# Three early operands of a mixed stage get buffers of their own, and the tiles around them move

## The chip, the cores and the metric

The kernel runs on one core of a Trainium2 chip. The metric is the device time of one execution in microseconds; lower is better. TensorE (PE) multiplies matrices into PSUM banks, VectorE (DVE), ScalarE (ACT) and GpSimd (POOL) work element by element, and SyncE (SP) and POOL issue transfers (DMA). The engines run their own programs in order and wait for each other by semaphores.

## The reference

```python
def reference(**kwargs):
    ...
    attn_out = _attn_ref(**attn_kwargs)
    B, H, S, D = attn_out.shape
    x = np.ascontiguousarray(attn_out.transpose(0, 2, 1, 3)).reshape(B * S, H * D)
    x = _moe_ref(x=x, **moe_kwargs)
    return _moe2_ref(x=x, **moe2_kwargs)
```

Attention here is a decaying linear state, `state = gamma * state + k v^T`, read with q, over 4 x 8 heads of 768 steps. Its 3072 rows of 512 go through `h = (x @ w1) * (x @ w2)`, `h @ w3`, `@ w_out`, and then through `h = x @ w_in`, `g = h * sigmoid(1.702 h)`, `g @ w_out`. All of it is float32.

## The kernel before

Every float32 product is made of three products of a reduced format: `mm3` multiplies high by high (L246), low by high (L247) and high by low (L248). The high part is a cast on ACT (L261, L132), the low part a subtraction on DVE (L162). Matrix products are also done by a scheme of seven products on 2 x 2 blocks, so the program has products P1 to P7 and sums of blocks. The program is written out by hand under `manual_schedule`: every engine runs in the order of the code. The tile pools hold SBUF addresses; where a new tile lies over older ones, its first writer waits for the last users of each of those tiles.

The order of stages is attention, with the first gates in it; the **gated blocks** (`ORDER = (0, 2, 4, 1, 3, 5)`, 8 steps `t` of 24 matmuls each), beside which the weights are mixed; the **mixed stage** (`blend`, 21 turns of 24 matmuls); **Expand**; and a contraction.

In the gated blocks n = 3 to 5, `gate_second` makes, for each pair of steps, `b12` and five quantities `g`, from two quantities `b` that an earlier block stored to `hd`. `b` is loaded with `load_b` (L1011), `g` is stored with `hd<-g` (L1027). DVE computes L1021 and L1024, POOL L1025 and L1026. In the last gated block, `opening(t)` also loads the first weights (`load_wm`) and the first operands of the mixed stage (`load_h`, tile names h0, h1), splits h0 and two weights into high and low.

In a turn of `blend`, PE multiplies operand n; ACT then makes the high part of operand n + 1 (`split_h`) and of the weight n + 2, and DVE the low parts; and `copied` on ACT takes finished banks (P1, P5, P6) into values `s`. P4's banks are copied to tiles "c" (tag `o`). POOL stores both to `yd`. Operands are loaded by `load_turn` (L796) three turns ahead. The pool of `blend` is named "c" and reuses addresses of the gated block. Expand's tiles (s, u, g, b) then reuse addresses of `blend`; its ACT copies at L551 take PE's banks a and e to s1, s5, u2 and so on.

Tile names carry a buffer number in the program's lists (`l_3865`); m, a, e and psm are PSUM banks.

Of the kernel before, what the change touches and what calls it, by code (L numbers as in the profile page):

```python
# [7 lines left out]
F32 = mybir.dt.float32  # L8
F32R = mybir.dt.float32r
# [7 lines left out]
P = 128  # L17
# [4 lines left out]
TB = 512  # L22
NB = NT // TB
# [3 lines left out]
R_BUFS = 5  # L27
# [10 lines left out]
NM = KF // 2  # L38
# [5 lines left out]
def tile_kernel(  # L44
# [242 lines left out]
    def h_tile():  # L287
        return xs.tile([P, 2, TB], F32, tag="h", bufs=2, name="h")
# [13 lines left out]
    class Attention:  # L302
# [9 lines left out]
        def tile(self, kind, n, bufs):  # L312
            return self.pool.tile([P, n], F32, tag=kind, bufs=bufs, name=kind)
# [479 lines left out]
    def load_h(n, a, b, t):  # L793
        i, name = blends[n]
        lo2.setdefault(n, []).append((a, b, t))
        nc.sync.dma_start(t.bitcast(F32), hd[i][:, a:b, RIGHT[name]])  # L796
# [13 lines left out]
    def split_wm(n):  # L810
        hi, lo = wm[blends[n][1]]
        split(hi, lo, lo.bitcast(F32))

    def load_wm(n):
        name = blends[n][1]
        wm[name] = wtile("wg")
        nc.sync.dma_start(wm[name][1].bitcast(F32), sm[PART[name]].rearrange("p k c -> p (k c)"))

    def opening(t):
        if t in range(1, 5):  # L820
            load_wm(t - 1)
        if t == 1:
            x = spare.tile([P, 7, TB], F32R, tag="ope", name="h0")
            hi2[0] = x[:, NM:]
            load_h(0, 0, NM, x[:, :NM])
        if t == KF - 2:
            for k in (0, 2):
                load_h(1, k, k + 2, prep.tile([P, 2, TB], F32R, tag="r", bufs=R_BUFS, name="h1"))
        if t in (3, 4, 5):
            split_h(0, t - 3, t - 2, hi2[0][:, t - 3 : t - 2])  # L830
        if t == 6:
            hi2["k3"] = prep.tile([P, TB], F32R, tag="x", bufs=6, name="h3")
            split_h(0, 3, 4, hi2["k3"].rearrange("p (a t) -> p a t", a=1))
        if t in (4, 6):
            split_wm(t // 2 - 2)

    def blend(p, ps, todo):
        ws = {}

        def tile(kind, bufs):  # L840
            return p.tile([P, NM, TB], F32R, tag=kind, bufs=bufs, name=kind)

        def load_turn(n):
            if n < len(blends):
                load_h(n, 0, NM, ls.pop(n) if n in ls else tile(f"l{n % 4}", 1))

        def value():
            return p.tile([P, TB], F32, tag="s", bufs=8, name="s")

        def copied(ps):  # L850
            t = ready.pop() if ready else value()
            nc.scalar.copy(t, ps)
            return t

        def store(i, e, t):
            nc.gpsimd.dma_start(yd[i][:, e], t)

        ls = {n: tile(f"l{n % 4}", 1) for n in range(2, 6)}
        load_turn(2)
        for n in range(4, 7):  # L860
            load_wm(n)
        load_turn(3)
        held = [p.tile([P, TB], F32, tag="o", bufs=2, name="c")]
        hi2[1] = tile("h", 2)
        ready = [value()]
        for n, (i, name) in enumerate(blends):
            if n < 7:
                ws[name] = [x.rearrange("p (k c) -> p k c", k=NM) for x in wm[name]]
            if n:
                load_turn(n + 3)  # L870
            if name == "P1":
                a, e, c = ([None] * 2 for _ in range(3))
                kept = [{}, {}]
            bank = dict(P5=e, P3=e, P2=c).get(name, a)
            for q in range(2):
                if name in ("P1", "P5", "P2"):
                    bank[q] = ps.tile([P, TB], F32, tag="m", bufs=8, name="m")
                for k in range(NM):
                    mm3(
                        bank[q],  # L880
                        *(x[:, k, q * P : (q + 1) * P] for x in ws[name]),
                        hi2["k3"] if (n, k) == (0, 3) else hi2[n][:, k],
                        low_h(n, k),
                        k == 0 and name in ("P1", "P5", "P2"),
                        k == NM - 1,
                    )
            if n == 7:
                left_tile(0)
                fetch_left(0)
            if n + 1 < len(blends):  # L890
                if n:
                    hi2[n + 1] = tile("h", 2)
                split_h(n + 1, 0, NM, hi2[n + 1])
            if n + 2 < 7:
                split_wm(n + 2)
            todo(n)
            for q, x in enumerate(kept):
                m = bank[q]
                if name in ("P1", "P5", "P6"):
                    x[name] = copied(m)  # L900
                if name == "P2":
                    nc.vector.tensor_tensor(x["P1"], m, x["P1"], ALU.add)
                    store(2 * i, q, x["P1"])
                if name == "P7":
                    nc.vector.tensor_tensor(x["P5"], m, x["P5"], ALU.add)
                    store(2 * i + 1, 2 + q, x["P5"])
                if name == "P3":
                    nc.vector.tensor_tensor(x["P6"], m, x["P6"], ALU.add)
                    store(2 * i + 1, q, x["P6"])
                if name == "P4":  # L910
                    t = held.pop() if held else p.tile([P, TB], F32, tag="o", bufs=2, name="c")
                    nc.scalar.copy(t, m)
                    store(2 * i, 2 + q, t)

    with tc.manual_schedule():
# [54 lines left out]
        with (  # L970
# [35 lines left out]

            hb = []

            def load_b(i, k):
                t = h_tile()  # L1010
                nc.sync.dma_start(t, hd[i // 2][:, k, :2])  # L1011
                hb.append(t)

            def gate_second(t, i, ab):
                nonlocal b12, g
                b = hb[0]
                if t % 2 == 0:
                    b12 = first_b.pop() if first_b else b12_tile()
                    g = pb.tile([P, 5, TB], F32, tag="g", bufs=2, name="g")
                    gate_out(b12, ab)  # L1020
                    nc.vector.tensor_tensor(g[:, 1], b12, b[:, 0], ALU.subtract)  # L1021
                    return
                gate_out(g[:, 0], ab)
                nc.vector.tensor_tensor(g[:, 3], g[:, 0], b12, ALU.subtract)  # L1024
                nc.gpsimd.tensor_tensor(g[:, 2], g[:, 0], g[:, 1], ALU.subtract)  # L1025
                nc.gpsimd.tensor_tensor(g[:, 4], b[:, 1], g[:, 2], ALU.subtract)  # L1026
                nc.gpsimd.dma_start(hd[i // 2][:, t // 2, 2:], g)  # L1027
                hb.pop(0)

            def b12_tile():  # L1030
                return pb.tile([P, TB], F32, tag="b", bufs=2, name="b12")
# [2 lines left out]
            for n, i in list(enumerate(ORDER))[1:]:  # L1034
                nxt = ORDER[n + 1] if n + 1 < NB else None
                for t in range(KF):
                    if nxt is None:
                        opening(t)
                    elif t < 2:
                        for d in range(2):  # L1040
                            reload(nxt, 2 * t + d)
                    if n > 2 and t % 2 == 0 and t + 2 < KF:
                        load_b(i, t // 2 + 1)
                    if n >= 2 and nxt is not None and t == KF - 2:
                        load_b(nxt, 0)
                    ab = gate_mm(t, i, gate_tile)
                    if nxt is not None and t in range(KD - 1, KF - 1):
                        split_x(nxt, t - KD + 1)
                    work(((8, 6, 3, 3)[n - 1] + (n < 4) * (t % 2)) if n < 5 else (t < 4) + (t < 5))
                    (gate_second if n > 2 else gate_first)(t, i, ab)  # L1050
                    while rows < KF and (complete > W3 + rows or (n, t) == (2, KF - 1)):
                        ps = mix_mm(rows)
                        work(7)
                        mix_out(rows, ps)
                        rows += 1
                        if rows == KF:
                            stage.close()
                            pb = homes["st"] = stage.enter_context(
                                tc.tile_pool(name="b2", bufs=1, reuse_waits="tile")
                            )  # L1060
                            st_ready = [pb.tile([P, 1024], F32, tag="st", bufs=2, name="st")]
                            first_b = [b12_tile()]
                            pb.tile([P, 1024], F32, name="gap")
        inner.close()
        homes["st"] = second.enter_context(
            tc.tile_pool(name="wa", bufs=1, side="right", reuse_waits="tile")
# [135 lines left out]
```

## Time and profile before

| what | value |
|---|---|
| median of three runs | 982.17 us (981.41 to 983.0) |
| span of the profiled execution, its own time | 982.2 us |
| PE busy | 963.9 us, 98% |
| DVE, ACT, POOL busy | 718.7, 443.9, 203.3 us |
| mean granted clock of PE | 0.998 |
| mixed stage begins, Expand begins | 397.06, 515.92 us |

The span is from the first to the last instruction of one profiled execution. It equals the median, so its times need no scaling.

### The profile page before, as it was taken

The page shows a single profiled execution, that of the slowest core. Times are in us where ns is not written, and L with a number is a line of the kernel's source. Part 1 is how long each engine was busy: PE and PEld are TensorE (multiplying, and loading weights), DVE is VectorE, ACT ScalarE, POOL GpSimd, SP SyncE. Part 2 cuts the span into 40 slices and gives each one's busy share as a digit, 9 for nine tenths or more (in the row PEclk, how much of TensorE's full clock was granted, in tenths as well). Part 3 has the DMA queues.
Part 4 walks back from the last instruction along what each step waited for, and adds up shares of the span by engine and source line. Part 5 has one row for each costly group of instructions (what it writes and reads, how often), then busy time and mean ns, then how long its engine had stood idle before and what let it go on. Part 6 is the DMA issues. An engine that isn't in the chain of part 4 may idle for free.

```text
span 982.2 us, 14858 instructions
## 1 busy us (share of the span) xinstructions
PE 963.9 (98%) x5608; PEld 835.2 (85%) x5608; DVE 718.7 (73%) x965; ACT 443.9 (45%) x787; POOL 203.3 (21%) x248
## 2 busy tenths in 40 slices
PE   7899999999999999999999999999999999999998
PEld 6788878888888888788889999999999888888886
DVE  4878878989898996765786895867777475567662
ACT  5666644443322222545536745444545544354430
POOL 5010000278685875250110000000000000000000
PEclk9999999999999999999999999999999999999999
DMA  9889965669998989979868647465596968767871
GB/s 362 347 325 355 354 208 192 220 232 346 319 318 324 347 316 356 402 254 322 269 233 296 242 176 278 174 235 223 202 360 253 331 227 282 244 192 251 288 236 54
DMA packets 115288, 268.73 MB, mean 274 GB/s; under 512 B 8000, under 2 KB 69440, under 8 KB 106128
## 3 DMA queue, kind: packets, MB, share of 16 engines
q1 hardware_dynamic: 100688, 193.98, 56.6%
q0 software_dynamic: 14384, 73.61, 19.2%
q8 instruction: 44, 0.72, 0.3%
q14 instruction: 28, 0.23, 0.1%
q10 hardware_dynamic: 144, 0.20, 0.1%
HBM read 165.52 MB, written 102.24 MB: 273 GB/s over the span
## 4 chain that ended last, share of the span: by engine, by line
PE 88%; DVE 5%; DMA 3%; ACT 2%; issue 1%; POOL 0%; DVEq 0%; ACTq 0%; POOLq 0%
PE m L247 11%; PE m L248 11%; PE m L246 11%; PE psm L246 7%; PE psm L247 7%; PE psm L248 7%; PE a L247 4%; PE a L248 4%; PE a L246 4%; PE e L248 2%; PE e L247 2%; PE e L246 2%; PE y L404 2%; PE s L354 2%; PE psg L246 1%
## 5 line engine op out<-in xcount | busy, mean ns | idle before, releaser
L246 PE MATMUL psm<-xh,wh 128*128 128x512 f32 x320 | 124.6, 389 | 0.0
L247 PE MATMUL psm<-xl,wh 128*128 128x512 f32 x320 | 124.5, 389 | 0.0
L248 PE MATMUL psm<-xh,wl 128*128 128x512 f32 x320 | 124.5, 389 | 0.0
L246 PE MATMUL m<-h,op 128*128 128x512 f32 x320 | 124.5, 389 | 0.0
L248 PE MATMUL m<-h,op 128*128 128x512 f32 x320 | 124.5, 389 | 0.0
L247 PE MATMUL m<-l,op 128*128 128x512 f32 x304 | 118.3, 389 | 0.0
L685 ACT CAST h<-l 128x2048 fp32r<-128x2048 f32 x38 | 72.3, 1914 | 83.0 <-PE m L248 58.0
L686 DVE TENSOR_TENSOR l<-l,h 128x2048 fp32r<-128x2048 f32 x38 | 85.6, 2286 | 20.7 <-ACT h L685 20.7
L247 PE MATMUL a<-yl,op 128*128 128x384 f32 x256 | 85.6, 334 | 0.1
L246 PE MATMUL a<-yh,op 128*128 128x384 f32 x256 | 85.6, 334 | 0.0
L248 PE MATMUL a<-yh,op 128*128 128x384 f32 x256 | 85.5, 334 | 0.0
L691 POOL DMA_DIRECT2D op<-sw x6 | 3.2, 533 | 393.2 <-PE a L248 212.9
L128 ACT ACTIVATE x<-raw 128x512 f32<-128x512 f32 x72 | 46.6, 672 | 76.1 <-DMA raw<-in_wo_dram 43.9
L246 PEld LDWEIGHTS psm<-xh,wh 128*128 128x128 f32 x320 | 60.1, 188 | 12.7 <-issue 0.2
L248 PEld LDWEIGHTS psm<-xh,wl 128*128 128x128 f32 x320 | 60.1, 188 | 12.5
L246 PEld LDWEIGHTS m<-h,op 128*128 128x128 f32 x320 | 60.1, 188 | 12.5
L248 PEld LDWEIGHTS m<-h,op 128*128 128x128 f32 x320 | 60.1, 188 | 12.4
L247 PEld LDWEIGHTS psm<-xl,wh 128*128 128x128 f32 x320 | 60.1, 188 | 12.3
L247 PEld LDWEIGHTS m<-l,op 128*128 128x128 f32 x304 | 57.1, 188 | 12.0
L246 PE MATMUL m<-h,wh 128*128 128x512 f32 x168 | 66.0, 393 | 0.6 <-ACT h L261 0.6
L248 PE MATMUL m<-h,wl 128*128 128x512 f32 x168 | 66.1, 393 | 0.0
L162 DVE TENSOR_TENSOR l<-l,h 128x2048 fp32r<-128x2048 f32 x19 | 43.5, 2291 | 29.8 <-ACT h L261 29.7
(165 smaller groups left out, 2209.3 us busy)
## 6 DMA issues: line engine op xcount, KB each, us to landing
gd<-g SPq DMA_DIRECT2D x32, 1344.0 KB, 4.7
qkv<-in_qkv_dram POOLq DMA_DIRECT2D x20, 1024.0 KB, 9.1
l<-gd SPq DMA_DIRECT2D x26, 768.0 KB, 6.9
l<-hd SPq DMA_DIRECT2D x19, 1024.0 KB, 7.8
raw<-in_w_dram SPq DMA_DIRECT2D x30, 512.0 KB, 5.1
hd<-g POOLq DMA_DIRECT2D x12, 1280.0 KB, 8.7
raw<-in_wo_dram SPq DMA_DIRECT2D x24, 512.0 KB, 7.5
l<-gd SPq DMA_DIRECT2D x24, 512.0 KB, 5.1
```

The costliest lines, as they stand in the source:

```text
L128: nc.scalar.activation(x, high, AF.Abs, scale=2.0**16)
L162: nc.vector.tensor_tensor(lo, x, hi.bitcast(F32), ALU.subtract)
L246: nc.tensor.matmul(ps, wh, xh, start=start, stop=False, skip_group_check=True)
L247: nc.tensor.matmul(ps, wh, xl, start=False, stop=False, skip_group_check=True)
L248: nc.tensor.matmul(ps, wl, xh, start=False, stop=stop, skip_group_check=True)
L354: nc.tensor.matmul(sc[c][j][:, p, :], qkt[c][r, 1, p, :], qkt[c][r, 0, p, :], start=True, stop=True,)
L404: nc.tensor.matmul(out_y, vs[c][:, 2 * p + j, :], pt[c][:, j, p, :], start=(p < 2), stop=first, skip_group_check=True,)
L685: nc.scalar.copy(hi, x.bitcast(F32))
L686: nc.vector.tensor_tensor(x, x.bitcast(F32), hi.bitcast(F32), ALU.subtract)
L691: queue.dma_start(t.bitcast(F32), sw[PART[name]])
```

## The change

- A pool "l" with three tiles is opened when the weight mixing ends. Operands of blends 1 to 3 go there, and later operands reuse it (`next_turn`). Their loads are issued at t = 4 of the last gated block. Before, blend 1's came at t = 6 in two halves and 2 and 3 at the start of `blend`.
- The weights of blends 4 to 6 are loaded at t = 5 to 7 rather than at the start of `blend`.
- `load_b` goes to POOL's queue, behind the store of each pair and two pairs ahead, save for the first two.
- In `blend`, P1's values get two tiles of their own (tag s1) and the others six; the order in which tiles are taken is another, and so are their addresses. A gap of 2432 elements instead of 1024 stands in the pool "b2" of the gated block, ahead of the two `g` tiles.

```diff
--- before.py
+++ after.py
@@ -823,9 +823,11 @@
             x = spare.tile([P, 7, TB], F32R, tag="ope", name="h0")
             hi2[0] = x[:, NM:]
             load_h(0, 0, NM, x[:, :NM])
-        if t == KF - 2:
-            for k in (0, 2):
-                load_h(1, k, k + 2, prep.tile([P, 2, TB], F32R, tag="r", bufs=R_BUFS, name="h1"))
+        if t == 4:
+            for n in range(1, 4):
+                load_h(n, 0, NM, next_turn(n))
+        if t in range(5, 8):
+            load_wm(t - 1)
         if t in (3, 4, 5):
             split_h(0, t - 3, t - 2, hi2[0][:, t - 3 : t - 2])
         if t == 6:
@@ -834,6 +836,10 @@
         if t in (4, 6):
             split_wm(t // 2 - 2)
 
+    def next_turn(n):
+        home = homes["l0" if n % 4 == 0 else "l"]
+        return home.tile([P, NM, TB], F32R, tag=f"l{n % 4}", name="l")
+
     def blend(p, ps, todo):
         ws = {}
 
@@ -842,27 +848,25 @@
 
         def load_turn(n):
             if n < len(blends):
-                load_h(n, 0, NM, ls.pop(n) if n in ls else tile(f"l{n % 4}", 1))
-
-        def value():
-            return p.tile([P, TB], F32, tag="s", bufs=8, name="s")
-
-        def copied(ps):
-            t = ready.pop() if ready else value()
+                load_h(n, 0, NM, first_l.pop() if n == 4 else next_turn(n))
+
+        def value(name):
+            tag, bufs = ("s1", 2) if name == "P1" else ("s", 6)
+            return p.tile([P, TB], F32, tag=tag, bufs=bufs, name="s")
+
+        def copied(ps, name):
+            t = ready.pop() if ready else value(name)
             nc.scalar.copy(t, ps)
             return t
 
         def store(i, e, t):
             nc.gpsimd.dma_start(yd[i][:, e], t)
 
-        ls = {n: tile(f"l{n % 4}", 1) for n in range(2, 6)}
-        load_turn(2)
-        for n in range(4, 7):
-            load_wm(n)
-        load_turn(3)
+        homes["l0"] = p
+        hi2[1] = tile("h", 2)
+        ready = [value("P1")]
+        first_l = [next_turn(4)]
         held = [p.tile([P, TB], F32, tag="o", bufs=2, name="c")]
-        hi2[1] = tile("h", 2)
-        ready = [value()]
         for n, (i, name) in enumerate(blends):
             if n < 7:
                 ws[name] = [x.rearrange("p (k c) -> p k c", k=NM) for x in wm[name]]
@@ -897,7 +901,7 @@
             for q, x in enumerate(kept):
                 m = bank[q]
                 if name in ("P1", "P5", "P6"):
-                    x[name] = copied(m)
+                    x[name] = copied(m, name)
                 if name == "P2":
                     nc.vector.tensor_tensor(x["P1"], m, x["P1"], ALU.add)
                     store(2 * i, q, x["P1"])
@@ -1006,10 +1010,12 @@
 
             hb = []
 
-            def load_b(i, k):
-                t = h_tile()
-                nc.sync.dma_start(t, hd[i // 2][:, k, :2])
-                hb.append(t)
+            def load_b(n, k, queue=nc.gpsimd):
+                n, k = n + k // NM, k % NM
+                if n < NB:
+                    t = h_tile()
+                    queue.dma_start(t, hd[ORDER[n] // 2][:, k, :2])
+                    hb.append(t)
 
             def gate_second(t, i, ab):
                 nonlocal b12, g
@@ -1026,6 +1032,7 @@
                 nc.gpsimd.tensor_tensor(g[:, 4], b[:, 1], g[:, 2], ALU.subtract)
                 nc.gpsimd.dma_start(hd[i // 2][:, t // 2, 2:], g)
                 hb.pop(0)
+                load_b(ORDER.index(i), t // 2 + 2)
 
             def b12_tile():
                 return pb.tile([P, TB], F32, tag="b", bufs=2, name="b12")
@@ -1039,10 +1046,10 @@
                     elif t < 2:
                         for d in range(2):
                             reload(nxt, 2 * t + d)
-                    if n > 2 and t % 2 == 0 and t + 2 < KF:
-                        load_b(i, t // 2 + 1)
-                    if n >= 2 and nxt is not None and t == KF - 2:
-                        load_b(nxt, 0)
+                    if n == 2 and t == KF - 2:
+                        load_b(n, NM, nc.sync)
+                    if n == 3 and t == 0:
+                        load_b(n, 1, nc.sync)
                     ab = gate_mm(t, i, gate_tile)
                     if nxt is not None and t in range(KD - 1, KF - 1):
                         split_x(nxt, t - KD + 1)
@@ -1055,12 +1062,15 @@
                         rows += 1
                         if rows == KF:
                             stage.close()
+                            homes["l"] = first.enter_context(
+                                tc.tile_pool(name="l", bufs=1, reuse_waits="tile")
+                            )
                             pb = homes["st"] = stage.enter_context(
                                 tc.tile_pool(name="b2", bufs=1, reuse_waits="tile")
                             )
                             st_ready = [pb.tile([P, 1024], F32, tag="st", bufs=2, name="st")]
                             first_b = [b12_tile()]
-                            pb.tile([P, 1024], F32, name="gap")
+                            pb.tile([P, 2432], F32, name="gap")
         inner.close()
         homes["st"] = second.enter_context(
             tc.tile_pool(name="wa", bufs=1, side="right", reuse_waits="tile")
```

What the addresses become: the tiles "l" lie at bytes 73856 to 98432 of each partition. `g` has two tiles at 120448 to 140928. In the pool "c", the values `s` of the other products lie at 131200 to 143488, over the second `g` tile, and the two "c" tiles at 127104 to 131200.

**The loads on SP in the last gated block.** SP before; h0, h1 and l are operands of blends, wl weights, L1011 the loads of b:

```order
L817 DMA wl_3765<-sm0_99 128x1024 [waits DMASW5_49,DMASW4_49,DMASW7_49,DMASW1_49,PE_49]
L1011 DMA h_3767<-hd2_79 128x1024 [waits DMAHW2_49,DMAHW4_49,DVE_49,Pool_49]
L817 DMA wl_3815<-sm0_99 128x1024 [waits DMAHW3_49,PE_49]
L817 DMA wl_3854<-sm0_99 128x1024 [waits PE_49]
L1011 DMA h_3860<-hd2_79 128x1024 [waits DMAHW5_49,DMAHW6_49,DVE_49,Pool_49]
L796 DMA h1_3928<-hd0_77 128x2x512 [waits DMASW7_49,DMASW3_49,Activation_49]
L796 DMA h1_3930<-hd0_77 128x2x512 [waits DMASW7_49,DMAHW7_49,DMASW3_49,Activation_49]
L796 DMA l2_4012<-hd0_77 128x4x512 [waits DMASW4_49,DMASW6_49,DMASW3_49,DMASW7_49,DMASW2_49,DMAHW0_49,DMASW1_49,DMASW0_49]
L817 DMA wl_4018<-sm0_99 128x1024 [waits DMAHW1_49,PE_49]
L817 DMA wl_4021<-sm0_99 128x1024 [waits DMAHW2_49,PE_49]
L817 DMA wl_4024<-sm0_99 128x1024 [waits DMAHW3_49,PE_49]
L796 DMA l3_4013<-hd0_77 128x4x512 [waits DMAHW4_49,DVE_49]
```

SP with the change:

```order
L796 DMA h0_3731<-hd0_77 128x4x512 [waits DMAHW0_49]
L817 DMA wl_3770<-sm0_99 128x1024 [waits DMASW5_49,DMASW7_49,DMASW4_49,DMAHW1_49,DMASW1_49,PE_49]
L817 DMA wl_3818<-sm0_99 128x1024 [waits DMAHW2_49,PE_49]
L817 DMA wl_3859<-sm0_99 128x1024 [waits DMAHW3_49,PE_49]
L796 DMA l_3861<-hd0_77 128x4x512 [waits DMASW3_49,DMASW5_49,DMASW2_49,DMAHW4_49,DMASW0_49,Pool_49]
L796 DMA l_3863<-hd0_77 128x4x512 [waits DMAHW5_49,DMASW6_49]
L796 DMA l_3865<-hd0_77 128x4x512 [waits DMAHW6_49]
L817 DMA wl_3904<-sm0_99 128x1024 [waits DMAHW7_49,PE_49]
L817 DMA wl_3941<-sm0_99 128x1024 [waits DMAHW0_49,PE_49]
L817 DMA wl_3980<-sm0_99 128x1024 [waits DMASW6_49,DMAHW1_49,DMASW4_49,PE_49]
L796 DMA l_4028<-hd0_77 128x4x512 [waits DMASW6_49,DMASW5_49,DMASW7_49,DMASW4_49,DMAHW2_49,DVE_49,Pool_49]
```

The load of blend 3 stood last of the rows before (`l3_4013`), behind a wait for DVE. The three loads of l now stand together behind the weights of the opening, and the loads of b are gone from this engine. The last row of the change is the load of blend 4, which waits for g and its store.

**The start of the mixed stage on ACT.** L852 copies a bank to a value, L261 casts an operand (h) or weight (wh). Before:

```order
L852 COPY s_4029<-m_4030 128x512 [waits PE_49]
L852 COPY s_4065<-m_4043 128x512 [waits PE_49,Activation_49]
L261 CAST h_4094<-l2_4012 128x2048 [waits DMAHW0_49]
L261 CAST wh_3853<-wl_3854 128x1024 [waits DMAHW4_49]
L852 COPY s_4101<-m_4068 128x512 [waits PE_49]
L852 COPY s_4103<-m_4081 128x512 [waits PE_49]
L261 CAST h_4130<-l3_4013 128x2048 [waits DMAHW4_49,DVE_49]
```

With the change (L859 is the same copy):

```order
L859 COPY s_4027<-m_4030 128x512 [waits PE_49]
L859 COPY s_4063<-m_4043 128x512 [waits PE_49]
L261 CAST h_4092<-l_3863 128x2048 [waits DMAHW5_49,DVE_49]
L261 CAST wh_3858<-wl_3859 128x1024 [waits DMAHW3_49]
L859 COPY s_4099<-m_4066 128x512 [waits DMASW5_49,PE_49,Pool_49]
L859 COPY s_4101<-m_4079 128x512 [waits PE_49,Activation_49]
L261 CAST h_4129<-l_3865 128x2048 [waits DMAHW6_49,DVE_49]
```

The first copy of P5 (`s_4099`; `s_4101` before) has gained a wait for DMASW5, which is the last store hd<-g, and POOL. The cast of blend 3's operand (last row) stands two rows behind it.

**The start of Expand on ACT.** L912 (L916) copies P4's banks of the last blend, L551 Expand's first banks. Before:

```order
L912 COPY c_4796<-m_4550 128x512 [waits DMASW6_49,PE_49]
L912 COPY c_4799<-m_4563 128x512 [waits DMASW7_49,PE_49]
L551 COPY s1_4829<-a_4834 128x384 [waits DVE_49,PE_49]
L551 COPY s5_4850<-e_4835 128x384 [waits DMASW3_49,DMASW4_49,DVE_49,PE_49]
L551 COPY u2_4858<-a_4834 128x384 [waits PE_49]
```

With the change:

```order
L916 COPY c_4795<-m_4549 128x512 [waits DMASW0_49,PE_49]
L916 COPY c_4798<-m_4562 128x512 [waits DMASW1_49,PE_49]
L551 COPY s1_4829<-a_4834 128x384 [waits DVE_49,PE_49]
L551 COPY s5_4850<-e_4835 128x384 [waits DMASW0_49,DMASW1_49,PE_49,Activation_49]
L551 COPY u2_4858<-a_4834 128x384 [waits PE_49]
```

The second copy (`s5_4850`) waited for DMASW3 and DMASW4, two earlier stores of yd. It now waits for DMASW0 and DMASW1, which are the stores of the two "c" tiles copied just above it.

## Rows read from the trace of the kernel before

**Rows 1.** The page's first lines: busy us, share of span, instructions.

```profile
span 982.2 us, 14858 instructions
...
PE 963.9 (98%) x5608; PEld 835.2 (85%) x5608; DVE 718.7 (73%) x965; ACT 443.9 (45%) x787; POOL 203.3 (21%) x248
```

**Rows 2.** Waits of PE, 200 to 470 us: total us, times, longest.

```profile
PE m L247 <- DVE l L162: 1.8, 1, 1.8
PE m L246 <- ACT h L261: 0.6, 1, 0.6
```

**Rows 3.** Chain of waits, 396 to 424 us: start, duration, what.

```profile
398.78 13.36 DMA l<-hd
...
414.15 2.30 DVE l L162
```

**Rows 4.** PE's timeline at 8 and from 396: start, duration, idle in brackets.

```profile
8.15 2.08 PE L354 MATMUL s<-qkv 64*128 64x128 f32 x16 [1.88 <-DMA qkv<-in_qkv_dram]
...
397.06 0.39 PE L246 MATMUL m<-h,wh 128*128 128x512 f32 x1
...
413.16 0.39 PE L248 MATMUL m<-h,wl 128*128 128x512 f32 x1
414.17 0.51 PE L246 MATMUL m<-h,wh 128*128 128x512 f32 x1 [0.62 <-ACT h L261]
416.50 0.69 PE L247 MATMUL m<-l,wh 128*128 128x512 f32 x1 [1.82 <-DVE l L162]
...
423.89 0.39 PE L248 MATMUL m<-h,wl 128*128 128x512 f32 x1
```

**Rows 5.** Windows: length, busy of five engines, granted clock, DMA share, GB/s.

```profile
8.00:9.00 1.00, 0.85 (x8) 0.85 (x10) 0.00 (x0) 0.57 (x3) 0.53 (x1) 1.00 1.05 369
...
417.00:418.00 1.00, 1.00 (x4) 0.81 (x3) 1.00 (x2) 1.00 (x2) 0.00 (x0) 0.50 1.02 375
419.00:420.00 1.00, 1.00 (x4) 0.71 (x4) 1.00 (x1) 0.00 (x0) 1.00 (x1) 0.50 0.04 16
420.00:421.00 1.00, 1.00 (x6) 0.83 (x5) 1.00 (x2) 0.00 (x0) 0.97 (x1) 0.98 0.00 0
```

**Rows 6.** ACT's timeline in the mixed stage.

```profile
403.24 1.92 ACT L261 CAST h<-l 128x2048 fp32r<-128x2048 f32 x1
...
414.97 1.06 ACT L852 COPY s<-m 128x512 f32<-128x512 f32 x2
```

**Rows 7.** POOL's timeline, the last store hd<-g.

```profile
402.43 0.57 POOL L1027 DMA_DIRECT2D hd<-g  x1 [0.30 <-POOL g L1026]
```

**Rows 8.** The line that stores hd<-g, then its last transfer.

```profile
DMA to landing us min/median/max: 7.6/8.7/10.8
...
hd<-g POOLq DMA_DIRECT2D x1, 1280.0 KB, 8.4
```

**Rows 9.** DVE's timeline, blend 1's low part in two halves.

```profile
398.67 4.55 DVE L162 TENSOR_TENSOR h<-h,h 128x1024 fp32r<-128x1024 f32 x2
```

**Rows 10.** Windows, 340 to 392 us, columns as in group 5.

```profile
340.00:392.00 52.00, 52.00 (x231) 43.07 (x230) 41.54 (x49) 12.51 (x21) 35.29 (x37) 1.00 0.90 331
```

**Rows 11.** PE's timeline, fifth product of Expand.

```profile
520.10 0.33 PE L246 MATMUL a<-yh,op 128*128 128x384 f32 x1
```

**Rows 12.** ACT's timeline at the start of Expand.

```profile
518.22 0.48 ACT L551 COPY s<-e 128x384 f32<-128x384 f32 x1 [0.56 <-PE e L248]
...
526.12 0.53 ACT L561 ACTIVATE g<-s 128x384 f32<-128x384 f32 x1 [1.18 <-DMA yd<-c]
```

**Rows 13.** POOL's last store yd<-c, yd stores, transfers issued 516.5 to 518.5.

```profile
517.00 0.54 POOL L856 DMA_DIRECT2D yd<-c  x1 [0.75 <-ACT c L912]
...
DMA to landing us min/median/max: 3.2/3.9/9.0
...
op<-sp SPq DMA_DIRECT2D x2, 896.0 KB, 10.6
yd<-c POOLq DMA_DIRECT2D x1, 256.0 KB, 9.0
```


## The prediction

> **What bounds the kernel now.** I read the page first: TensorE (PE) is busy for 963.9 of the 982.2 us [rows 1]. Any gain or loss must therefore show as an idle or slow stretch of PE, and an edit elsewhere counts only if PE waits for it. The waits of PE come next. From 200 us to 470 us it waits for something other than its own sequencer just twice: 1.8 us for the low part (VectorE, DVE, L162) and 0.6 us for the high part (ScalarE, ACT, L261) of one operand of the mixed stage [rows 2]. The chain of waits names the cause: a load of `l` from `hd` that only started at 398.78 and took 13.36 us, then a cast, then the 2.30 us subtraction [rows 3]. It is the load of blend 3, whose buffer lay under tiles of the gated block.
>
> What that stall costs is read from PE's timeline [rows 4]. The stage starts at 397.06. 71 matmuls later it is 413.16, so one takes 16.10/71 = 0.2268 us. The matmul at 423.89 is 98 after the first and would start at 397.06 + 98 x 0.2268 = 419.28 without a stall. **The stall costs 4.6 us**: about 2.9 of lateness up to the second L247, and the rest because the granted clock fell to 0.50 (1.2 GHz) from 417 to 420, back at 0.98 in the next microsecond [rows 5]. It fell after two idles close together; after a lone idle of 1.88 us [rows 4] the clock stayed at 1.00 [rows 5].
>
> **The change part by part.**
>
> *Early loads of blends 1 to 3: -4.6 us.* Their buffers are now a pool of their own, opened after the mixing, and all three loads leave SP at t = 4 of the last gated block, about 365 us. With 3 MB more in that stretch, whose DMA engines are busy 0.90 of the time at 331 GB/s [rows 10], they land well before turn 3 at 413. The old stall goes, all 4.6 us.
>
> *New wait 1, in the mixed stage: +3.3 us (0 to 5.9).* The values' buffers move up over `g`. The first P5 value, `s_4099`, now lies over the second `g` tile, so its copy waits for the last store hd<-g. Behind it on ACT stand the other copy and the cast of turn 3's operand (the second piece of order). The store was issued at 402.43 [rows 7] and its landing took 8.4 us, of 7.6 to 10.8 over all twelve [rows 8]. I call the landing X. Then come two copies (1.06 us for the pair), the cast, 1.91 [rows 6], and the subtraction, 2.30 [rows 3], with some 0.15 of gaps: turn 3's low part is ready at X + 5.4 us. PE wants it with the second matmul of turn 3, at 397.06 + 73 x 0.2268 = 413.6. So the idle is X - 408.2. Fewer loads run beside the store than before (the two of 1 MB at that time are gone, one of blend 4 comes), so I put the landing between the fastest of the twelve and the old one: X = 402.4 + 8.1 = 410.5, **idle 2.3**. The floor: a 256 KB store landed in 3.2 us [rows 13], and the further 1.05 MB, at the 331/0.90 = 368 GB/s that fully busy DMA engines would move [rows 10], adds 2.8: X = 408.4 and next to no idle. The ceiling: the old 8.4 after an issue up to 1.7 us later, since the single DVE subtraction of blend 1's operand runs beside GpSimd's (POOL's) last operation: X = 412.5, idle 4.3. For the clock I add 1.0, between none (as after the lone 1.88) and the 1.7 of the old stall: 2.3 + 1.0 = 3.3.
>
> The Trainium skill, "DMA: Bandwidth & Descriptors", section "Anatomy of one DMA - SWDGE (gpsimd) path", gives a transfer issued from GpSimd as about 2.0 us plus its bytes over 436 GB/s. By that fit this store would take an estimated 5.0 us and wait 1 would be nothing; the twelve stores of this trace took 7.6 to 10.8 [rows 8], beside other transfers, and I go by them.
>
> *New wait 2, at the start of Expand: +8.6 us (1.2 to 10).* The `c` tiles of P4 move up too, and Expand's second copy, `s5_4850`, now lies over them. It waits for both last stores yd<-c (the third piece of order); before, it waited for older stores that had landed, and ran at 518.22 [rows 12]. The last yd<-c is issued at 517.00, and took 9.0 us although it is only 256 KB: two loads op<-sp, of 896 KB each and 10.6 us to landing, were queued beside it [rows 13]. The old trace shows when it was done: ACT's gate function at 526.12 waited for yd<-c [rows 12]. So s5 starts at 526.1, and the copy behind it, `u2`, ends at 526.1 + 2 x 0.48 = 527.05. PE's next product into that bank (520.10 before [rows 11]) needs u2 and starts then: **idle 6.95**. An idle this long I price with the full clock loss of the old stall, 1.65: 8.6. Everything queued behind (the next cast of op, the gate functions, DVE) shifts along; PE has no slack later to take it back, being busy 98%. The floor is a landing in 3.2 us, the fastest of the yd stores [rows 13]: 520.2, u2 at 521.2, 1.2 us and no clock loss. The ceiling is a landing 1.4 us later.
>
> By the fit cited above a store of 256 KB would take an estimated 2.6 us, and this wait would cost about 0.6 us at most; the trace's 9.0 [rows 13] speaks against it here. What follows from a fast landing is the third rival below.
>
> *b from POOL's queue: 0.* Each load moves behind the store hd<-g on POOL, about two pairs ahead of its use. An issue costs POOL about 0.57 us [rows 7], some 12 times, and POOL is busy 35.3 of 52 us in that stretch [rows 10]. The load starts later by the store's 1.3 MB, some 2 to 3 us, and the DVE operation that wants it with it. But PE is full throughout (52.00 of 52.00), with six PSUM banks, enough for three steps of 24 x 0.2268 = 5.44 us ahead of the gate, which covers 16 us. Without that cover it would be up to 3 us once per pair; a gain is excluded, since PE waits for nothing there.
>
> *h1 in one piece: 0.* Blend 1's high and low parts are made by one operation each and not by two halves. DVE's two halves ended at 403.2 [rows 9]; turn 1 starts at 402.50, so PE may wait up to 0.5 us there. That would only be taken off wait 1, which is bound by X and not by PE.
>
> **Sum.** The profiled execution spans 982.2 us, which is the median of the three runs (982.17), so no correction. 982.2 - 4.6 + 3.3 + 8.6 = **989.5 us**.
>
> **The rivals.**
>
> 1. *Only wait 2 bites.* Fewer loads beside the last hd<-g let it land in under 6 us, so X is below 408.3. For it: the pair of 1 MB loads that ran beside it is gone. Against: not one of twelve took less than 7.6, and in most stretches the DMA engines are full. 982.2 - 4.6 + 8.6 = 986.2; with part of wait 1, up to 988.
>
> 2. *The stores land fast, and the kernel gets faster.* The 9.0 us of the last yd<-c came from its place among the op<-sp loads; the median of the eight yd stores is 3.9 [rows 13]. If the loads are issued some us apart from it, it lands at 520 to 521 and wait 2 costs 1.1 to 2. With wait 1 at 0.8 the time is 982.2 - 4.6 + 0.8 + 1.1 = 979.5. It decides the sign when both waits together stay under 4.6 us, which with wait 1 as forecast means a landing before about 521.4. For it: six yd stores landed near 3 to 4 us. Against: the op<-sp loads depend on the same releases as before, and nothing in the change moves them. With no new wait at all, 977.6.
>
> 3. *Both waits at their ceilings*, or a queue behind the 3 MB of earlier loads that delays `b` or the weights beyond PE's cover: 982.2 - 4.6 + 5.9 + 10 = 993.5.
>
> **How the numbers follow.** Forecast (both waits, within 986.8 to 992.8): 0.62. First rival (984.8 to 986.8): 0.22. Second (under 984): 0.10. Third (above 992.8): 0.06. The likeliest case gives the time, 989.5. The range from 984.6 to 992.8 leaves out the second and third rivals, 0.16, and a little of the first. About 0.2% (2 us) is what a measurement of this kernel can tell from no change. Of the second rival most lies under 980.2 and the rest within 2 us of before: faster 0.08, same 0.04, slower 0.88.
>
> **What would show it.** In the profile after, PE's waits from 200 to 470 should have no load of `l` behind them; turn 3 should instead wait about 2 us for ACT and DVE, with the copy of `s_4099` released by the store hd<-g at about 410.5. In Expand, ACT's second copy should be released by yd<-c at about 526 less what the stage gained, and PE idle about 7 us before its fifth product, with the granted clock near 0.50 for some 3 us behind it. PE should be full from 340 to 392. The forecast is wrong if yd<-c lands within 4 us of its issue, if PE waits in the last gated blocks for `b`, or if X is under 408.

## The result and the profile after

The changed kernel takes 992.74 us (median of six runs, 989.65 to 995.17) against 982.59 us for the kernel before (981.28 to 983.71): a ratio of 1.0115, with a 95% interval from 1.0096 to 1.0134. It is slower, as forecast, and by more: 10.15 us where the sum gave 7.3. In the measure of the three runs that the prediction started from, 1.0115 x 982.17 is 993.5 us, outside the range that ended at 992.8.

The page of the profile after, to be read against [rows 1]:

```profile
span 991.8 us, 14837 instructions
...
PE 965.1 (97%) x5608; PEld 836.6 (84%) x5608; DVE 716.9 (72%) x964; ACT 443.6 (45%) x786; POOL 209.5 (21%) x258
```

This execution took 993.59 us by the clock that gives the times, so 1.8 us lie outside the span. The span grew by 9.6 us and PE's busy time by 1.2. Behind attention, the waits of PE (total, times, longest) name two places:

```profile
PE a L246 <- ACT u L551: 6.6, 1, 6.6
...
PE m L247 <- DVE l L162: 1.8, 1, 1.8
...
PE m L246 <- ACT h L261: 0.9, 1, 0.9
```

The load of `l` is gone as a cause. The wait in turn 3, which answers to [rows 2], is still there, and the one in Expand is new. PE's timeline, to be read against [rows 4] and [rows 11], with the first matmul of the mixed stage, the two that wait in turn 3, the first of Expand and the one that waits there:

```profile
397.82 0.39 PE L246 MATMUL m<-h,wh 128*128 128x512 f32 x1
...
415.24 0.50 PE L246 MATMUL m<-h,wh 128*128 128x512 f32 x1 [0.94 <-ACT h L261]
417.57 0.50 PE L247 MATMUL m<-l,wh 128*128 128x512 f32 x1 [1.82 <-DVE l L162]
...
517.02 0.33 PE L246 MATMUL a<-yh,op 128*128 128x384 f32 x1
...
527.94 0.69 PE L246 MATMUL a<-yh,op 128*128 128x384 f32 x1 [6.56 <-ACT u L551]
```

Who released them is read on ACT's timeline: the copies of P5's two values, then the cast of turn 3's operand; then Expand's second and third copies ([rows 6, 12]):

```profile
412.32 1.07 ACT L859 COPY s<-m 128x512 f32<-128x512 f32 x2 [5.51 <-DMA hd<-g]
413.27 1.91 ACT L261 CAST h<-l 128x2048 fp32r<-128x2048 f32 x1
...
527.02 0.48 ACT L551 COPY s<-e 128x384 f32<-128x384 f32 x1 [8.26 <-DMA yd<-c]
527.40 0.48 ACT L551 COPY u<-a 128x384 f32<-128x384 f32 x1
```

Both copies ran late because they waited for a store: 5.51 us of idle up to the landing of hd<-g, 8.26 us up to that of yd<-c. The chain of waits has this transfer, from its issue:

```profile
518.10 8.82 DMA yd<-c
```

The places add up. The mixed stage runs from 397.82 to 517.02, 119.20 us, where [rows 4] and Expand's start at 515.92 gave 118.86: +0.34. Expand and all behind it take 991.8 - 517.02 = 474.8 us, where it was 466.3: +8.5. The last 0.76 us were lost before 397, in the mixing of the weights, where one matmul waited 0.97 us for a low part, and 0.20 in the profile before:

```profile
175.10 0.50 PE L248 MATMUL psw<-wh,wl 128*128 128x512 f32 x1 [0.97 <-DVE wl L137]
```

```profile
174.34 0.50 PE L248 MATMUL psw<-wh,wl 128*128 128x512 f32 x1 [0.20 <-DVE wl L137]
```

A second profile of the changed kernel (`change_again`, below) has 0.20 there too, so this is a matter of the execution and not of the change. 0.34 + 8.5 + 0.76 = 9.6.

The windows (length, busy of five engines, granted clock, DMA share, GB/s) answer to [rows 5, 10]:

```profile
419.00:420.00 1.00, 1.00 (x4) 0.76 (x4) 1.00 (x2) 0.85 (x1) 0.61 (x1) 0.53 0.00 0
...
421.00:422.00 1.00, 1.00 (x3) 0.75 (x3) 1.00 (x2) 0.00 (x0) 1.00 (x1) 0.50 0.00 0
422.00:423.00 1.00, 1.00 (x5) 0.77 (x4) 1.00 (x1) 0.00 (x0) 0.92 (x2) 0.76 0.00 0
...
521.00:527.00 6.00, 0.38 (x3) 0.05 (x1) 0.00 (x0) 0.00 (x0) 0.00 (x0) 0.82 1.01 400
...
530.00:531.00 1.00, 1.00 (x5) 1.00 (x5) 1.00 (x1) 0.48 (x1) 0.00 (x0) 0.50 0.00 0
532.00:533.00 1.00, 1.00 (x8) 1.00 (x7) 0.93 (x2) 0.00 (x0) 0.00 (x0) 1.00 0.00 0
...
340.00:392.00 52.00, 52.00 (x231) 43.05 (x230) 43.34 (x50) 12.73 (x21) 39.29 (x42) 1.00 0.95 356
```

The granted clock fell to 0.50, 1.2 GHz, with both waits: for about 3 us behind the idles of turn 3, and in Expand already within the idle (a mean of 0.82 from 521 to 527) and until past 531. In the last line PE is full from 340 to 392 as before, with the DMA share at 0.95 instead of 0.90: the early loads and `b` on POOL's queue cost nothing there.

### The profile page after: what moved, and what is told of

It is laid out like the page before. It is cut to its first block, busy times and chain, and to the rows that moved or that the text cites. A ratio compares the mean times of both kernels' runs of the same rounds, so it can differ in the third digit from the quotient of the medians.

```text
span 991.8 us, 14837 instructions
## 1 busy us (share of the span) xinstructions
PE 965.1 (97%) x5608; PEld 836.6 (84%) x5608; DVE 716.9 (72%) x964; ACT 443.6 (45%) x786; POOL 209.5 (21%) x258
## 5 line engine op out<-in xcount | busy, mean ns | idle before, releaser
L686 DVE TENSOR_TENSOR l<-l,h 128x2048 fp32r<-128x2048 f32 x38 | 85.6, 2285 | 20.8 <-ACT h L685 20.8
L162 DVE TENSOR_TENSOR l<-l,h 128x2048 fp32r<-128x2048 f32 x20 | 46.9, 2345 | 30.2 <-ACT h L261 30.1
```

What stands on the lines that cost most here:

```text
L162: nc.vector.tensor_tensor(lo, x, hi.bitcast(F32), ALU.subtract)
L686: nc.vector.tensor_tensor(x, x.bitcast(F32), hi.bitcast(F32), ALU.subtract)
```

## The experiments

**Moving the tiles apart.** Three kernels have every load, queue and order of the change, and only other addresses in the pool "c" (and, in two, of `g`). P5's values get a tag of their own, so that they can be placed (two tiles for P5 and four for the rest, where the change has six for both):

```diff
-            tag, bufs = ("s1", 2) if name == "P1" else ("s", 6)
+            tag, bufs = {"P1": ("s1", 2), "P5": ("s5", 2)}.get(name, ("s", 4))
...
-            t = ready.pop() if ready else value(name)
+            t = ready.pop(name) if name in ready else value(name)
...
-        ready = [value("P1")]
+        ready = {"P1": value("P1")}
         first_l = [next_turn(4)]
+        ready["P6"] = value("P6")
         held = [p.tile([P, TB], F32, tag="o", bufs=2, name="c")]
+        ready["P5"] = value("P5")
...
-                            pb.tile([P, 2432], F32, name="gap")
+                            pb.tile([P, 2048], F32, name="gap")
```

This is the third of them, `both_moved`. In `c_moved` the order of the tags is P6, P5, "c" and the gap stays at 2432; in `p5_moved` it is "c", P6, P5 with the gap of 2048.

> Only the addresses in the pool c differ from the change: P4's tiles c stand last (139392 to 143488), out of the way of Expand's first copies; both P5 values still lie over the second g tile. Theory (two waits for stores, each by an overlap of tiles): the 6.6 us idle of PE in Expand and the low clock behind it go, 8.5 us in all, and the wait in turn 3 stays: about 984.3 us against 992.7 for the change and 982.6 for before. Rival (the loads moved forward and b on POOL's queue crowd the transfers, and the stores are only where it shows): PE waits for something else near there, and the time stays above 989 us.

Measured: 984.77 us (980.42 to 986.75, ten runs), the kernel before on the same chip 980.08; ratio 1.0035 (1.0015 to 1.0054). Its PE waits near the change are those of turn 3 alone:

```profile
PE m L247 <- DVE l L162: 1.8, 1, 1.8
...
PE m L246 <- ACT h L261: 0.9, 1, 0.9
```

> Only addresses differ from the change: the g tiles start 1536 bytes lower, and the two P5 values have tiles of their own above them (139392 to 143488). P4's tiles c still lie under Expand's second copy. Theory: the wait in turn 3 goes (2.8 us idle and some 2.1 us of low clock, 4.9 in all), the wait in Expand stays: about 987.8 us. If the landing of the last store hd<-g were not what ACT waited for, PE would still idle in turn 3 and the time would stay at 992 to 993 us.

Measured: 988.46 us (988.23 to 988.80); ratio 1.0085 (1.0064 to 1.0105). The one wait there is Expand's:

```profile
PE a L246 <- ACT u L551: 6.9, 1, 6.9
```

> Both address edits together: P5 values off g, P4's tiles c off Expand's first copies; all loads, their queues and their order are those of the change. Theory: PE never waits in the mixed stage nor at the start of Expand, and what is left is the gain of the early loads: 992.7 - 4.9 - 8.5 = about 979.3 us, 3.3 us faster than before (4.6 if nothing else costs). Rival (crowding): the time is not under that of before, 982.6 us.

Measured: 979.29 us (979.01 to 980.87, ten runs); ratio 0.9982 (0.9967 to 0.9997). PE waits nowhere from the first matmul of the mixed stage to the first of Expand:

```profile
397.16 0.39 PE L246 MATMUL m<-h,wh 128*128 128x512 f32 x1
...
511.40 0.33 PE L246 MATMUL a<-yh,op 128*128 128x384 f32 x1
```

That is 114.24 us, 504 matmuls at 0.2267. All three landed within 0.7 us of what the two-wait theory said, and crowding by itself, the rival, is out: with the same transfers and no overlap nothing is lost. By the medians on this chip wait 1 costs 984.77 - 979.29 = 5.5 us, wait 2 costs 988.46 - 979.29 = 9.2 us. But the gain over before was 0.8 us here and not 3.3, because before itself was faster, and it spread over 979.0 to 984.7 in 19 runs.

**The change and before again.** Neither kernel is altered.

> The changed kernel once more, unaltered, as the reference for the other kernels on this chip, since before measured 980.1 us in the last runs and not 982.6. Theory (before's old stall costs 0 to 5 us from one execution to the next, the change's two waits are there in all): about 992 us again, some 11 us over before. Rival (the chips differ by a constant): 990 us.

Measured: 992.40 us (990.27 to 996.10); ratio 1.0113 (1.0085 to 1.0141) to 981.26 for before. The change costs as much on this chip as in its first runs. Its profile shows wait 1 in another size, though (PE's timeline, then a window with the columns as above):

```profile
397.12 0.39 PE L246 MATMUL m<-h,wh 128*128 128x512 f32 x1
...
413.95 0.50 PE L246 MATMUL m<-h,wh 128*128 128x512 f32 x1 [0.34 <-ACT h L261]
416.27 0.50 PE L247 MATMUL m<-l,wh 128*128 128x512 f32 x1 [1.82 <-DVE l L162]
...
514.08 0.33 PE L246 MATMUL a<-yh,op 128*128 128x384 f32 x1
```

```profile
418.00:419.00 1.00, 1.00 (x6) 0.84 (x5) 1.00 (x1) 0.56 (x1) 0.91 (x1) 1.00 0.08 31
```

The mixed stage takes 514.08 - 397.12 = 116.96 us, 2.7 more than the 114.24 without a stall, where the first profile of the same kernel had 5.0: the last store hd<-g landed 7.4 us after its issue and not 8.0, the first idle was shorter, and the granted clock stayed at 1.00 behind the two. Expand and all behind it take 989.6 - 514.08 = 475.5 us, 9.2 more than the 466.3 without a wait. So wait 1 differs from one execution to the next, as the old stall does.

> The kernel before once more with a profile. Its times on the last chip lay from 979.0 to 984.7, those of the version with both edits from 979.0 to 980.9. Theory: the load of blend 3's operand lands early enough in some executions for PE not to wait in turn 3. A profile with a short span (977 to 978) shows PE without that wait, one with a long span (over 981) shows it. Rival: the variation is at the start or in the contraction.

Measured: one run, 979.47 us, span 977.7. The kernel *before* has no stall in this execution: its timeline has the same two rows as that of `both_moved`, the first matmul of the mixed stage at 397.16 and the first of Expand at 511.40.

114.24 us again. The cast of blend 3's operand on ACT was held up until 412.21 by its load ([rows 3]) in the profile that the prediction was read from; here it followed straight on the work before it, and the load took 6.6 us instead of 13.4:

```profile
412.21 1.90 ACT L261 CAST h<-l 128x2048 fp32r<-128x2048 f32 x1 [3.48 <-DMA l<-hd]
```

```profile
408.72 1.92 ACT L261 CAST h<-l 128x2048 fp32r<-128x2048 f32 x1
...
l<-hd SPq DMA_DIRECT2D x1, 1024.0 KB, 6.6
```

The load was issued at the same point in both, 398.78 and 398.87.

So the old stall is a matter of the execution: 4.6 us in the one that the prediction was read from, nothing in this one. This span equals that of `both_moved`, so the change without its two waits is worth just the old stall, whatever that was.

**What sets the landing of hd<-g.** First the halves of blend 1's operand:

> One edit to the change: blend 1's operand is split in two halves again, as before. It asks why the last store hd<-g was issued at 404.27 - 0.76 = 403.5 us on the clock of before and not at 402.4: POOL's last operation took 3.22 us beside DVE's one long subtraction, 2.15 before. If that is so, it takes about 2.2 us again, the store is issued and lands some 1.1 us earlier, and PE's idle in turn 3 shrinks from 2.8 us to about 1.7: 991 to 991.8 us, within what can be told from the change only by the trace. Rival: the 3.22 us come from something else (three loads beside it), and POOL's operation stays above 3 us.

```diff
-                split_h(n + 1, 0, NM, hi2[n + 1])
+                for k in (0, 2) if n == 0 else (0,):
+                    m = 2 if n == 0 else NM
+                    split_h(n + 1, k, k + m, hi2[n + 1][:, k : k + m])
```

Measured: 994.37 us (992.86 to 994.83); ratio 1.0142 (1.0120 to 1.0164). POOL's last operation and the store, with the change (and DVE's long subtraction beside them) and then with the halves:

```profile
400.74 3.22 POOL L1032 TENSOR_TENSOR g<-h,g 128x512 f32<-128x512 f32 x1
404.27 0.57 POOL L1033 DMA_DIRECT2D hd<-g  x1 [0.31 <-POOL g L1032]
...
399.42 3.38 DVE L162 TENSOR_TENSOR l<-l,h 128x2048 fp32r<-128x2048 f32 x1
```

```profile
399.94 2.15 POOL L1034 TENSOR_TENSOR g<-h,g 128x512 f32<-128x512 f32 x1
402.39 0.57 POOL L1035 DMA_DIRECT2D hd<-g  x1 [0.31 <-DMA wl<-sm]
```

The first half of the expectation held: 2.15 us and not 3.22, and the store left 1.1 us earlier for the stage's start. The second failed: it landed no earlier, and PE idled for 3.6 us in turn 3 (1.75 and 1.82) and not 1.7. The transfers that it shared the engines with, first in the change (issues of 402 to 405, KB each and us to landing), then with the halves (402 to 408, with POOL's queue in these 6 us ahead of them: packets, MB, share; the second of the two loads was issued at 407.9):

```profile
hd<-g POOLq DMA_DIRECT2D x1, 1280.0 KB, 8.0
l<-hd SPq DMA_DIRECT2D x1, 1024.0 KB, 6.4
```

```profile
q0 software_dynamic: 15, 0.15, 6.0%
...
l<-hd SPq DMA_DIRECT2D x2, 1024.0 KB, 7.6
hd<-g POOLq DMA_DIRECT2D x1, 1280.0 KB, 9.8
```

With the halves POOL's queue moved 0.15 MB in these 6 us although the store was issued at 402.39. The 1 MB load of blend 4, released by the store of the pair before, had left just ahead of it. So the store was put ahead of that load:

> One edit to the change: the load of blend 4's operand (1 MB) goes to POOL's queue, behind the last store hd<-g; before, SP issued it about 1 us ahead of that store. It asks what set the landing at 412.2 both in the change and with the halves, though the store was issued 1.1 us earlier there. Theory (the store stands behind the 1 MB load in the DMA engines): it lands some 2.5 us earlier, near 409, PE's idle in turn 3 falls from 2.8 to under 1 us, the clock stays up, and the time falls by 3 to 4.5 us against the change, to about 988.5. Rival (the store's own 1.3 MB takes 8 us): no change.

```diff
-        nc.sync.dma_start(t.bitcast(F32), hd[i][:, a:b, RIGHT[name]])
+        queue = nc.gpsimd if n == 4 else nc.sync
+        queue.dma_start(t.bitcast(F32), hd[i][:, a:b, RIGHT[name]])
```

Measured: 989.61 us (989.18 to 990.09); ratio 1.0082 (1.0064 to 1.0100), 2.8 us less than the change on the same chip. POOL's queue in the same 6 us, the store, and PE's wait in turn 3:

```profile
q0 software_dynamic: 123, 1.26, 61.9%
...
hd<-g POOLq DMA_DIRECT2D x1, 1280.0 KB, 5.8
```

```profile
414.63 0.50 PE L247 MATMUL m<-l,wh 128*128 128x512 f32 x1 [0.88 <-DVE l L162]
```

The store lands in 5.8 us, and the wait for the low part is halved. The mixed stage takes 512.50 - 397.04 = 115.5 us here, so 1.2 us of wait 1 are left, where the profile of `change_again` has 2.7. The gain is a little under what was expected.

**What sets the landing of yd<-c.** In the change, SP issued three loads op<-sp at 517.22, 517.63 and 518.12, beside the last store's issue at 518.10:

```profile
op<-sp SPq DMA_DIRECT2D x3, 896.0 KB, 9.6
```

> One edit to the change: the last three loads op<-sp go to POOL's queue, where they stand behind the two last stores yd<-c. Theory (the store of 256 KB takes 9 us because three loads of 896 KB were issued just ahead of it): the store lands in 3 to 4 us, about 522; PE's idle at Expand's start shrinks from 6.6 us to 1 to 2 with no low clock, and the time falls by 6 to 7.5 us against the change, to about 985.5. Rival (a store from POOL's queue to that place is slow in itself): the store takes 8 us or more again and the time stays.

```diff
-                fetch_left(n, nc.sync)
+                fetch_left(n, nc.sync if n < 4 else nc.gpsimd)
```

Measured: 981.93 us (980.84 to 987.09, ten runs); ratio 1.0019 (0.9999 to 1.0039). The landings (min, median, max) of the stores to yd, and PE's wait:

```profile
DMA to landing us min/median/max: 2.7/3.5/3.8
```

```profile
518.37 0.44 PE L246 MATMUL a<-yh,op 128*128 128x384 f32 x1 [0.70 <-ACT u L551]
```

The slowest store to yd takes 3.8 us here and took 8.8 with the change. The time fell by 10.5 us, more than expected: by the spans, Expand and what follows take 980.3 - 513.33 = 467.0 us, so 0.7 of wait 2 is left of the 9.2 that `change_again` has. The mixed stage takes 513.33 - 396.96 = 116.4 us here, so wait 1 is 2.1 against 2.7. These two make 9.1 of the 10.5; that wait 1 was shorter still in other runs of the ten, and longer in the three of 986.5 to 987.1, is likely but no profile shows it.

**The queue of b.**

> One edit to the change: the loads of b go back to SP's queue, at the place in the program where the change has them on POOL's. Theory (b's queue costs nothing, since PE is full beside it): PE waits in turn 3 and in Expand as with the change, and the time is that of the change, 992.5 us within 1.5. Rival (b behind 1.3 MB of stores on POOL's queue delays the last store hd<-g, or the loads for the mixed stage): the last store is issued or lands over 1 us earlier than with the change, and the time falls by 2 us or more.

```diff
-            def load_b(n, k, queue=nc.gpsimd):
+            def load_b(n, k, queue=nc.sync):
```

Measured: 993.63 us (992.52 to 994.97); ratio 1.0118 (1.0089 to 1.0147). PE's waits are those of the change:

```profile
PE a L246 <- ACT u L551: 6.8, 1, 6.8
...
PE m L247 <- DVE l L162: 1.8, 1, 1.8
...
PE m L246 <- ACT h L261: 1.1, 1, 1.1
```

The queue of `b` is no part of the matter.

## Why the prediction was wrong, point by point

- **The mechanisms and the sign: right.** Early loads remove the old stall; `s_4099` waits for hd<-g and Expand's second copy for yd<-c. Each wait alone came with its overlap and went without it.
- **Wait 2, +8.6: right.** 8.5 in the first profile, 9.2 by the medians; idle 6.56 for 6.95, with the clock down for longer than was counted. Its cause is shown too: the loads op<-sp issued just ahead of the store and with it, as the trace of before suggested.
- **Wait 1, +3.3: mis-sized.** It is 119.20 - 114.24 = 5.0 us in the first profile. What the prediction calls idle is the lateness of turn 3's low part: 417.57 - (397.82 + 73 x 0.2268) = 3.2 us, for 2.3. The store took 8.0 us, for 8.1, but it left 1.1 us later on the stage's own clock, a cost that the prediction named only for its ceiling. The other 1.8 us are the clock's, where it says "I add 1.0", halfway between none and the old stall's 1.7. So the two terms missed by about as much each. Two idles close together of 0.94 and 1.82 are the old pair of 0.62 and 1.82 over again; the row nearest to the case was the old stall itself. But 5.0 is no fixed price either: in the profile of `change_again` the pair was 0.34 and 1.82, the clock stayed up, and wait 1 was 2.7, under the 3.3 of the forecast.
- **"The span equals the median, so no correction": wrong.** 1.8 us of every execution lie outside the span (993.59 against 991.8). The profiled execution of before with its 982.2 us span was thus one of about 984.0 us, above all three runs that were shown. The sum of 989.5 was a span, and as a time it would have been 991.3, with a range that ends at 994.6.
- **-4.6 for the early loads: right for that execution only.** A stall-free before takes 979.47, so the median before already held less of the old stall: 982.59 - 979.3 = 3.3 us in the first runs and 0.8 in those of the tile experiments. The last two points are one error with two faces: the profiled execution had more stall than the median, by about the amount that was left outside the span. With 979.4 as stall-free time, 5.0 and 8.5 give 992.9; 992.74 was measured.
- **b on POOL and blend 1 in one piece, 0: right in the sum**, shown by `b_sync` and `halves`. The one-piece operation did delay the store, but not its landing.
- **The rivals.** The first, wait 1 nearly vanishing, is what three of the ten runs of `c_moved` look like (980.4 to 980.7, 1.1 to 1.4 us above `both_moved`); they have no profile, but the store's landing does differ between profiles: 8.0 us in the first of the change, 7.4 in `change_again`, 6.7 in `op_behind`. The fast landing of the second rival was seen only where the loads stand behind the store, in `op_behind`. Its bound, "a landing before about 521.4", is 1 us too late: u2 ends 0.96 us behind the landing, so the bound is 520.4. Nothing else in the sum rests on it.

The Trainium skill's fit for a transfer issued from GpSimd ("DMA: Bandwidth & Descriptors", section "Anatomy of one DMA - SWDGE (gpsimd) path") gave estimates of 5.0 us for the 1.3 MB store and 2.6 for the 256 KB one. With the loads put behind them, the first took 5.8 us and the eight of the second size 2.7 to 3.8; with loads of about 1 MB ahead, the last of each took 8.0 and 8.8. The traces agree with it roughly for a store with no such load ahead, and the prediction was right to go by the rows beside other transfers.

The old stall was put down to a load that "only started at 398.78". The late start alone doesn't make it: issued at 398.87, the same load took 6.6 us in `before_again` and PE waited nowhere. In that profile the load of blend 2 ahead of it had been issued 3.2 us earlier (383.59 against 386.82). That this is why it landed sooner was not tried, so the cause of the spread stays open.

## What to carry to other kernels

When a pool is laid out anew, go through the first writer of each tile and ask which transfer still reads the addresses below it; a store issued in the last microseconds of a stage was the dangerous one here, both times, and moving tiles of 2 KB per partition can be worth more than the load that it was moved for (5.5 and 9.2 us here, for a gain of 0.8 to 3.3). Compare the profiled execution's own time, not its span, with the median before taking a stall from it as typical, and take a second profile where runs differ. And price a small store's landing by what is issued just ahead of it: here it was 3 us or 9.

## What the runs showed of the hardware that was not expected

- A store on POOL's queue that was issued 1.1 us earlier landed no earlier (9.8 us for 8.0, one profile each): a 1 MB load on SP's queue was ahead of it, and POOL's queue moved 0.15 MB in 6 us. With that load behind the store on the same queue, the queue moved 1.26 MB in these 6 us, and the store landed in 5.8.
- DVE's subtraction beside POOL's operation took 3.38 us as one 128x2048 piece (`after`), and 4.55 as two of 128x1024 (`halves`); POOL's operation beside it took 3.22 and 2.15. What the one gained the other paid.
- The granted clock stayed at 1.00 through PE's idle of 1.78 us in turn 3 of `op_behind`'s profile (mean 1.000 over the program), and through the pair of 0.34 and 1.82 in that of `change_again`; it fell to 0.50 after the pair of 0.94 and 1.82 in the first profile of the change, and after that of 0.62 and 1.82 in the profile before.
